# Linear attention and GEGLU on one core: attention's queries turned by VectorE through DRAM, every down projection by seven products, the attention chunks moved

## The chip, the core and the metric

The kernel runs on one core of a Trainium2 chip. The metric is the device time of one execution in microseconds (us). An execution has a span, from the first to the last instruction that the profiler records on the core, and a little time around it. The core has five engines that run side by side, each through its own list of instructions in order: TensorE (PE, matrix products; its weight loads stand as PEld), VectorE (DVE), ScalarE (ACT), GpSimd (POOL) and SyncE (SP). Here SP issues all the DMA transfers, in one queue. [...]

## The reference

x is 2048 tokens by 512 features, float32.

```
xn  = layernorm(x)
q, k, v = split(xn @ wqkv)              # 32 heads of 16
pq, pk  = phi(q), phi(k)                # phi(t) = (t + 1 if t > 0 else exp(t)) + 1e-6
kv  = sum over tokens of pk^T v, z = sum over tokens of pk      # per head
s   = ((pq @ kv) / (pq . z + 1e-6)) @ wo
g   = silu((gelu(xn @ w_gate) * (xn @ w_up)) @ w_down)          # 1792 hidden columns
out = x + s * g
```

## The kernel before

**Precision and tiles.** A float32 product is made from two rounded parts of each factor, high and low: three matrix products (high by high, high by low, low by high) stand for one. `split` makes the parts: ACT copies the high part, DVE (or POOL) subtracts it to leave the low part. Nearly every matrix instruction is a 128x128 weight tile against 512 columns. Most products are made block by block, two by two, with seven products in place of eight (`PRODUCTS`, `prod`, `fprod`, `down_strassen`); the sums and differences that this takes are made by DVE and POOL.

**Stages.** First a QKV stage over the 16 token tiles: layer norm, a transposition of xn by PE, k and q by seven products (the first four tiles by the plain sum), phi, and G = xn^T pk in four PSUM banks (`gps`), from which kv follows later. phi(q) goes to DRAM (`q_d`); the forms of xn for tokens 0 to 1023 go to DRAM too (`xh_d`, `xl_d`), those for tokens 1024 to 2047 stay (`Xh`, `Xl`). Then pass 1 (tokens 1024 to 2047) and, after the attention, pass 0 (tokens 0 to 1023) of the feed-forward net. A pass has seven units of 256 hidden columns. A unit has two quads, gate and up (`quad`): 42 matrix instructions each, into the banks FX, FY and FZ. The weights of a quad (`w`) are cut into their parts once, in pass 1 (`prep_w`), written to DRAM (`w_d`), and loaded from there in pass 0. The products h of units 0 to 4 go through the down projection by seven products (`down_strassen`, keys "E", banks dX, dY and dZ, 42 instructions a unit), with four differences of h (`h_sums`) and seven high and low pairs (`hfh`, `hfl`) a unit. Units 5 and 6 (`SD = 5`) go through a plain sum at the end of the pass (`down`, keys "D", bank d, 48 instructions a unit).

**Attention** stands between the passes, in four chunks of 512 tokens (`attn`). kv and M = kv @ wo are made there (`pkv`, `pm`, `M_hi`, `M_lo`), from G that came back from DRAM. For each of 16 token tiles phi(q) is loaded, POOL multiplies it by z (`u`), DVE sums by head (`den`), adds, takes the reciprocal (`rr`) and scales (`pn`); PE transposes it by products with the identity (`ptq`, 4 instructions for each of 16 pieces); ACT and DVE split it (`pqT`); PE makes s (`sps`, 12 instructions a tile, 16 tiles). Two chunks are multiplied by pass 1's silu there and go out, two go to DRAM (`s_d`) for the end of pass 0.

**The order of the work** isn't the order of the code. Each operation is recorded with its engine, a stated cost and what it reads and writes (`Plan.do`). The order of the matrix products is written out as a list of keys (`pe_keys`); `Plan.order` then simulates the engines with the stated costs, takes for each engine the operation with the earliest latest-start (`late`), and applies the drawn changes of `late` that the table `KEPT` names. What it emits is a fixed list for each engine. Nearly every line in the profile is that of a helper: L486 is any matrix product, L453 any copy of ACT, L459 any `tt` of DVE or POOL, L1024 an addition to `acc`, L449 any DMA.

## Time and profile before

| | |
|---|---|
| three runs | 611.77, 613.39 and 614.51 us; median 613.39 |
| the profiled execution | 613.08 us, of it the span 611.3 |
| PE busy | 604.2 us in 2736 matrix instructions |
| DVE, ACT, POOL busy | 464.9, 334.2 and 211.7 us |
| DMA | 112.70 MB, mean 184 GB/s |

How to read it: matrix instructions overlap in PE, so that one lasts about 390 ns by its row while the next begins 227 ns after it. Busy time counts a stretch in which several overlap once. An idle time stands beside the engine that had it, with what ended it; idle time of an engine that nobody waits for costs nothing. In rows of instructions, `out<-in` names the tiles, buffer numbers left out.

### The profile page before, as it was taken

The numbers are of one execution on the slowest core, as the hardware profiler recorded it, in microseconds if no ns is written. First come the engines' busy times: TensorE is split into PE (matmuls) and PEld (weight loads), VectorE is DVE, ScalarE is ACT, GpSimd is POOL, SyncE is SP. The second block draws the span as 40 slices with busy tenths as digits, with TensorE's granted clock in tenths as the row PEclk, the third lists the DMA queues.
The fourth block names the chain that finished last, engine by engine and source line by source line (L and its number), as shares of the span: only waits on it lengthen the run. The fifth ranks groups of instructions, "written<-read, shape, count | busy, mean of one in ns | idle before, by whom it ended". The sixth has DMA issues, their size and how long they took to land.

```text
span 611.3 us, 7799 instructions
## 1 busy us (share of the span) xinstructions
PE 604.2 (99%) x2736; PEld 497.0 (81%) x2736; DVE 464.9 (76%) x745; ACT 334.2 (55%) x602; POOL 211.7 (35%) x209
## 2 busy tenths in 40 slices
PE   9999999999999999999999999999999999999997
PEld 8887888888888888888888787888887888888886
DVE  6999888677799999999757698714566868686456
ACT  6787877786677464656343322244654535353533
POOL 4456754364453654543013324013031121300110
PEclk9999999999999999999999999999999999999999
DMA  7149921107838354481669795255534344343245
GB/s 260 54 144 310 282 86 57 48 36 293 322 123 328 105 240 159 185 304 71 246 233 397 287 399 198 87 189 192 205 102 174 117 158 154 122 154 122 71 168 192
DMA packets 49079, 112.70 MB, mean 184 GB/s; under 512 B 3088, under 2 KB 24848, under 8 KB 45456
## 3 DMA queue, kind: packets, MB, share of 16 engines
q1 hardware_dynamic: 49040, 112.21, 50.3%
q8 instruction: 21, 0.34, 0.2%
q14 instruction: 18, 0.15, 0.1%
HBM read 67.63 MB, written 44.56 MB: 184 GB/s over the span
## 4 chain that ended last, share of the span: by engine, by line
PE 92%; DVE 5%; DMA 1%; issue 1%; ACT 0%; POOL 0%; SPq 0%; ACTq 0%; POOLq 0%
PE FX L486 24%; PE FZ L486 12%; PE dX L486 9%; PE gps L486 7%; PE d L486 7%; PE FY L486 6%; PE X L486 6%; PE dZ L486 4%; PE Z L486 3%; PE sps L486 3%; PE dY L486 2%; PE k L486 2%; PE q L486 2%; PE Y L486 1%; PE pt L651 1%; PE warm L516 1%
## 5 line engine op out<-in xcount | busy, mean ns | idle before, releaser
L486 PE MATMUL FX<-Xh,w 128*128 128x512 f32 x448 | 134.8, 390 | 0.2 <-ACT fu L453 0.2
L1065 POOL TENSOR_TENSOR h<-h,g 128x512 f32<-128x512 f32 x28 | 38.6, 1377 | 185.2 <-DVE h L459 185.2
L486 PEld LDWEIGHTS FX<-Xh,w 128*128 128x128 f32 x448 | 83.8, 188 | 18.5 <-ACT fu L453 1.3
L486 PE MATMUL FX<-Xl,w 128*128 128x512 f32 x224 | 69.0, 389 | 0.0
L486 PE MATMUL FZ<-Xh,w 128*128 128x512 f32 x224 | 69.0, 389 | 0.0
L453 ACT COPY fu<-FX 128x512 f32<-128x512 f32 x56 | 32.8, 585 | 37.1 <-PE FX L486 36.1
L486 PEld LDWEIGHTS FX<-Xl,w 128*128 128x128 f32 x224 | 42.1, 188 | 8.8
L486 PEld LDWEIGHTS FZ<-Xh,w 128*128 128x128 f32 x224 | 42.1, 188 | 8.7
L1024 DVE TENSOR_TENSOR acc<-acc,dX 128x512 f32<-128x512 f32 x52 | 35.4, 680 | 15.9 <-PE dX L486 15.9
L459 DVE TENSOR_TENSOR h<-fu,FZ 128x512 f32<-128x512 f32 x28 | 19.2, 686 | 30.0 <-ACT fu L453 24.1
L459 POOL TENSOR_TENSOR sums<-draw 128x256 f32<-128x256 f32 x20 | 19.8, 1002 | 51.1 <-DMA draw<-in_B_w_down 27.4
L459 POOL TENSOR_TENSOR tmp<-raw 128x256 f32<-128x256 f32 x28 | 24.6, 889 | 36.2 <-ACT g L989 10.4
L459 POOL TENSOR_TENSOR u<-q,zacc 128x512 f32<-128x512 f32 x16 | 20.8, 1318 | 44.3 <-DMA q<-q_d 31.6
L486 PE MATMUL FZ<-Xl,w 128*128 128x512 f32 x112 | 34.5, 389 | 0.0
L486 PE MATMUL FY<-Xh,w 128*128 128x512 f32 x112 | 34.4, 390 | 0.0
L729 POOL TENSOR_TENSOR zacc<-zacc,kp 128x512 f32<-128x512 f32 x16 | 24.7, 1542 | 27.2 <-DVE kp L718 26.9
L486 PE MATMUL sps<-pqT,M_hi 128*128 128x512 f32 x128 | 32.3, 393 | 0.0
L453 ACT CAST hfh<-sums 128x512 fp32r<-128x512 f32 x40 | 24.3, 621 | 14.1 <-DVE sums L459 13.9
L453 ACT CAST hfh<-h 128x512 fp32r<-128x512 f32 x30 | 18.5, 622 | 24.1 <-DVE h L459 16.3
L486 PE MATMUL dX<-hfh,dh 128*128 128x512 f32 x80 | 31.2, 390 | 0.2 <-ACT dY L453 0.2
L486 PE MATMUL dX<-hfl,dh 128*128 128x512 f32 x80 | 31.2, 390 | 0.0
L459 DVE TENSOR_TENSOR hfl<-sums,hfh 128x512 fp32r<-128x512 f32 x40 | 31.0, 786 | 0.2
(198 smaller groups left out, 1514.6 us busy)
## 6 DMA issues: line engine op xcount, KB each, us to landing
w_d<-w SPq DMA_DIRECT2D x14, 1792.0 KB, 8.5
w<-w_d SPq DMA_DIRECT2D x14, 1792.0 KB, 7.3
draw<-in_B_w_down SPq DMA_DIRECT2D x14, 512.0 KB, 4.3
x<-in_A_x SPq DMA_DIRECT2D x16, 256.0 KB, 3.6
q_d<-qp SPq DMA_DIRECT2D x16, 256.0 KB, 2.1
q<-q_d SPq DMA_DIRECT2D x16, 256.0 KB, 7.6
xh_d<-Xh SPq DMA_DIRECT2D x4, 896.0 KB, 5.3
xl_d<-Xl SPq DMA_DIRECT2D x4, 896.0 KB, 7.2
```

The lines of the kernel that those rows point to most:

```text
L453: do("ACT", act(n, src.psum), lambda o, i: nc.scalar.copy(o, i), dst, src, name=name)
L459: do(eng, c, lambda o, p, q: getattr(e, f"tensor_{op}")(o, p, q), dst, a, b, name=name)
L486: nc.tensor.matmul(o if r is None else o[:, r], a, b, start=first, stop=made == self.passes[r], skip_group_check=self.on or r is not None)
L516: nc.tensor.matmul(o, w, w, start=True, stop=True)
L651: nc.tensor.transpose(o[:, k, :], a[:, k * P:(k + 1) * P], b)
L729: do("POOL", pool(D), lambda o, i: nc.gpsimd.tensor_add(o, o, i), zacc, p0, name="zacc")
L1024: do("DVE", dve(D), lambda o, i: nc.vector.tensor_add(o, o, i), o, ps, name="acc")
L1065: do("POOL", pool(NC), lambda o, i: nc.gpsimd.tensor_mul(o, o, i), h, g, name="h")
```

## The change

It has these parts.

- **q turned by DVE.** phi(q) is written to DRAM with its columns regrouped (the host permutes the q columns of wqkv), so that a tile that is read back has its four quarters of the features in four groups of 32 partitions. After the scaling (`pn`), one DVE instruction transposes the 32x32 squares of a tile (`turn`, a STREAM_TRANSPOSE that writes every fourth element) into a part of the tile `sums`, and a DMA writes it to `t_d`; a chunk is read back from there already turned (`tq`, `pql`, `pqh`). The 64 `ptq` products are gone. The z product, the sums by head and the reciprocals (`den`, into `rall`) are made earlier, and q is loaded twice, once for `den` and once for `turn`. These jobs have due times (`behind`, `DUE`): six `den` and four `turn` in pass 1, ten and twelve in pass 0.
- **All down sums by seven products.** `SD`, `down` and the plain sum are gone; units 5 and 6 of both passes go through `down_strassen`. POOL makes the low parts of unit 6's down weights (`EASED`).
- **The chunks.** One attention chunk (chunk 2) stands between the passes, and its s goes to DRAM; chunks 3, 0 and 1 follow pass 0, mixed at first with its last down products (`between`). Seven down products of pass 1 are moved into the start of pass 0 (`MOVED`). silu of pass 1 goes to DRAM (`g_d`) and is loaded again at the end.
- **kv and M early.** wv and wo are loaded at the start of pass 1, G stays on the chip, kv is made after the first quad's products and M just behind; M's parts go to DRAM (`m_d`) and are loaded twice, before each place that uses them.
- **Three quads' weights early.** Those of quads 11, 12 and 13 are cut in the QKV stage (`prep_early`), written to DRAM, and loaded in pass 1 as they are in pass 0.
- **The table `KEPT`** is another one, with more draws.

The diff, cut to its core (of `KEPT` one line each; the code of kv, M, silu and the loads of X is moved more than changed):

```diff
 KEPT = [
-    (-1, 12, [9000067, 9000070, 9000075, 9000095, 9000115]),
...
+    (100, 115, [30000012, 30000014]),
...
+            if o.due is not None:
+                o.late = min(o.late, o.due)
...
-    q_d = dram_view([S, D], "q_d", NT)
-    s_d = dram_view([D, S // 2], "s_d", NT // 2)
-    g_d = dram_view([P, KT, D], "g_d", KT)
-
-    w_d = dram_view([2 * (F // P // 2), P, 2 * 14 * P], "w_d", 2 * (F // P // 2))
+    q_d = dram_view([NT, KT, P, P], "q_d", NT)
+    g_d = dram_view([D, S // 2], "g_d", NT // 2)
+    t_d = dram_view([KT, P, S], "t_d", NT)
+    s_d = dram_view([D, NC], "s_d", KT)
+    m_d = dram_view([2, P, KT, D], "m_d", 2 * KT)
+
+    w_dram = dram.tile([2 * (F // P // 2), P, 2, 14, P], F32, name="w_d")
+    w_res = [[Res() for _ in range(8)] for _ in range(2 * (F // P // 2))]
+
...
-        dma(q_d(t, slice(t * P, (t + 1) * P)), phi(v, t, "q"), 256)
+        dma(q_d(t, t).map(lambda ap: ap.rearrange("q s e -> s q e")),
+            phi(v, t, "q").map(lambda ap: ap.rearrange("p (q e) -> p q e", e=P)), 256)
...
+    def prep_early(q):
+        raw, t = sums_w(q, R0)
+        for g, src in enumerate(sources(raw, t)):
+            n = GROUPS[g].stop - GROUPS[g].start
+            v = raw_tile(R1, f"we{q}{g}", [P, 2, D]) if g % 2 else None
+            f = [(half(v, hl) if v else tile_in("up", 34 + hl, [P, D], F32, f"we{q}{g}{hl}")).map(
+                lambda ap, n=n: ap.bitcast(F32R).rearrange("p (s c) -> p s c", c=P)[:, 0:n]) for hl in range(2)]
+            split(*f, src, n * P, f"w{g}")
+            for hl in range(2):
+                dma(w_d(q, hl, GROUPS[g], g), f[hl].map(lambda ap: ap.bitcast(F32)), 2 * n * 32)
+
+    EARLY = range(11, 14)
+    WHEN = (90, 140)
+    for n, q in enumerate(EARLY):
+        plan.due = WHEN[0] + (WHEN[1] - WHEN[0]) * n / len(EARLY)
+        prep_early(q)
...
+
+    rall = tile_in("cpool", "zacc", [P, NT, H], F32, "rall", NT)
+
+    def rden(t):
+        return rall.part(rall.res[t:t + 1], (slice(None), t))
+    def den(p, t):
+        q = U("qz", [35], f"qz{t}")
+        dma(rows_of(q), q_d(t, t).map(lambda ap: ap.rearrange("q (s i) e -> (q s) i e", i=KT)), 256)
+        do("POOL", pool(D), lambda o, z: nc.gpsimd.tensor_mul(o, o, z.unsqueeze(1).to_broadcast([P, KT, P])), rows_of(q), zq, name="u")
+        r = rden(t)
+        do("DVE", 0.59, lambda o, i: nc.vector.tensor_reduce(o, i, axis=AX.X, op=ALU.add), r, heads(q), name="den", port=False)
+        do("DVE", 0.11, lambda o, i: nc.vector.tensor_add(o, o, i), r.map(lambda ap: ap.rearrange("p (s h) -> p s h", s=KT)),
+           den_eps.map(lambda ap: ap.unsqueeze(1).to_broadcast([P, KT, H // KT])))
+        do("DVE", 0.28, lambda o: nc.vector.reciprocal(o, o), r, port=False)
...
+        for l, base, w in ((wv, 10, wqkv_k[:, c, 2 * D:3 * D]), (wo_sb, 14, wo[c * P:(c + 1) * P, :])):
+            l.append(tile_in("up", base + c, [P, D], F32, f"wvo{base}{c}"))
+            dma(l[c], ext(w), 256)
+    kv4 = tile_in("up", 18, [P, KT, P], F32, "kv4")
+    pkv = bank(5, "pkv", (P, KT, P))
+    for g in range(KT):
+        def run_kv(o, *ab, g=g):
+            for c in range(KT):
+                nc.tensor.matmul(o[:, g, :], ab[c][:, g * P:(g + 1) * P], ab[KT + c][:, g * P:(g + 1) * P],
+                                 start=(c == 0), stop=(c == KT - 1))
+        do("PE", 0.9, run_kv, pkv, *wv, *GT, key=("kv", g))
+    do("DVE", dve(D), lambda o, i, m: nc.vector.tensor_mul(o, i, m.unsqueeze(1).to_broadcast([P, KT, P])),
+       kv4, pkv, mask2)
+    for g in range(KT):
+        pm = bank([6, 7, 5, 6][g], f"pm{g}")
+        do("PE", 0.9, lambda o, a, b, g=g: nc.tensor.matmul(o, a[:, g, :], b, start=True, stop=True),
+           pm, kv4, wo_sb[g], key=("m", g))
+        m = [tile_in("up", 19 + 2 * g + hl if g < 2 else 25 + 2 * g + hl, [P, D], F32R, f"m{hl}{g}") for hl in range(2)]
+        split(*m, pm, D, "M")
+        for hl in range(2):
+            dma(m_d(KT * hl + g, (hl, slice(None), g)), m[hl].map(lambda ap: ap.bitcast(F32)), 256)
+
+    down_f = w_down.rearrange("(f p) n -> p f n", p=P)
+    FE, FC, FG = range(0, 3), range(3, 6), range(6, 10)
...
+        if q in EARLY:
+            w = ws[q] = tile_in("wp", ring("w", [0, 1, 2]), [P, 2, 14, P], F32R, f"w{q}", 8)
+            dma(w.map(lambda ap: ap.bitcast(F32)), w_d(q), 2220)
+            return
...
+            split(*f, src, n * w, "d", "POOL" if (p, u) in EASED else "DVE")
...
+    def turn(p, t):
+        pn = U("qz", [35], f"q{t}")
+        dma(rows_of(pn), q_d(t, t).map(lambda ap: ap.rearrange("q (s i) e -> (q s) i e", i=KT)), 256)
+        do("DVE", 0.6, lambda o, j: nc.vector.scalar_tensor_tensor(
+            o, o, EPS, j.unsqueeze(2).to_broadcast([P, H, DH]), op0=ALU.add, op1=ALU.mult),
+           heads(pn), rden(t), name="pn")
+        s = spare(p)
+        v = s.part(s.res[8:9], (slice(None), 6)).map(lambda ap: ap.rearrange("p (g c) -> p g c", c=P))
+        do("DVE", 0.6, lambda o, i: nc.vector.transpose(
+            o.rearrange("p g (s t) -> p g t s", t=KT), i.rearrange("p (t g d) -> p g t d", t=KT, d=32)),
+           v, pn, name="turn", port=False)
+        dma(t_d(t, (slice(None), slice(None), slice(t * P, (t + 1) * P))).map(lambda ap: ap.rearrange("g p c -> p g c")), v, 256)
+
...
+    def attn(c, M, place):
+
+        src = View([t_d(t, ()).res[0] for t in range(4 * c, 4 * c + 4)],
...
+                dma(tq[h], src[:, 2 * h:2 * h + 2], 512)
+            tq = [v[:, k] for v in tq for k in range(2)]
+        else:
+            tq = place(0, KT).map(lambda ap: ap.bitcast(F32))
+            dma(tq, src, 1024)
+            tq = [tq[:, k] for k in range(KT)]
         forms_ = []
         for k in range(KT):
-            pt = bank(ring("spt", [0, 1]), f"ptq{c}{k}", (P, 4, P))
-
-            def run_t(o, b, *a, k=k):
-                for j in range(4):
-                    nc.tensor.transpose(o[:, j, :], a[j][:, k * P:(k + 1) * P], b)
-            do("PE", 0.45, run_t, pt, ident, *pns, key=("QT", i, k))
-            ptf = pt.map(lambda ap: ap.rearrange("p j c -> p (j c)"))
-            f = [tile_in("up", places[i % 2][k][hl], [P, NC], F32R, f"pqT{hl}{c}{k}") for hl in range(2)]
-            split(*f, ptf, NC, "pqT")
+            f = [place(KT + 2 * k + hl, 1)[:, 0] for hl in range(2)]
+            split(*f, tq[k], NC, "pqT", "POOL" if c in HELPED else "DVE")
             forms_.append(f)
         for n in range(KT):
-            ps = bank(ring("sps", [3, 4, 2]), f"sps{c}{n}")
-            Sum(ps).add(("S", i, n), *three([[M[hl].part(M[hl].res[k:k + 1], (slice(None), k, slice(n * P, (n + 1) * P))) for hl in range(2)]
-                                             for k in range(KT)], forms_), name="S")
...
+            ps = bank(ring("sps", [3, 4, 2, 0, 1]), f"sps{c}{n}")
+            Sum(ps).add(("S", c, n), *three([[m[:, k, rows] for m in M] for k in range(KT)], forms_), name="S")
+            if c == CHUNKS[0]:
+                so = U("so", FG, f"so{n}")
+                copy("ACT", so, ps, D, "so")
+                dma(s_d(n, rows), so, 256)
+                continue
+            out_tile(c, n, ps)
...
+                g = acc[0, 4 * c + n]
+                silu(g)
             else:
-                so = U("sxr", FACC, f"so{c}{n}")
...
+    def between(p, wait, s):
+
+        out = wait + down_keys(p, NU - 1)
+        for n, (k, at_) in enumerate(zip(s, BETWEEN[p])):
+            out.insert(at_ + n, k)
+        return out
...
+    BETWEEN = {1: (7, 9, 11, 14), 0: (5, 8, 11, 14)}
+    DENS = 6
+    HELPED = (2,)
+    EASED = ((1, 6), (0, 6))
+    MOVED = 7
+    DUE = {1: (150, 320), 0: (355, 530)}
...
+    behind(1, *DUE[1], *[(den, t) for t in TURN[:DENS]], *[(turn, t) for t in TURN[:4]])
...
+    g_take(100)
+    pe_keys += keys[2:5] + ["z"] + keys[5:KV] + [("kv", g) for g in range(KT)] + keys[KV:KV + 3]
+    pe_keys += [("m", g) for g in range(KT)] + keys[KV + 3:]
+    middle = between(1, wait, sums(CHUNKS[0]))
+    moved = middle[len(middle) - MOVED:]
+    pe_keys += middle[:len(middle) - MOVED]
...
+    behind(0, *DUE[0], *[(den, t) for t in TURN[DENS:]], *[(turn, t) for t in TURN[4:]])
+    keys, wait = ffn(0, moved)
+    M = load_m()
+    vs = {hl: tile_in("xf", hl, [P, 14, NC], F32R, f"pq{hl}", 14) for hl in "lh"}
+    for n in range(KT):
+        s = U("g", SPOTS, f"s{n}")
+        dma(s, s_d(n, at(0, n)[0]), 256)
+        out_tile(CHUNKS[0], n, s)
+    for c, hl in zip(CHUNKS[1:], "lhl"):
+        attn(c, M, lambda i, n, v=vs[hl]: v.part(v.res[i:i + n], (slice(None), slice(i, i + n))))
+    pe_keys += keys + between(0, wait, sums(CHUNKS[1])) + sums(CHUNKS[2]) + sums(CHUNKS[3])
```

What PE does between the last quad of pass 1 and the first of pass 0. Before, the plain sums' last tile (d), the transpositions (ptq) and the first attention products (sps):

```order
L486 MATMUL d_5_70_3477<-hh_11_3133,dwh_3068 128x512
L486 MATMUL d_5_70_3477<-hh_11_3058,dwh_3043 128x512
L1241 MATMUL ptq_3523<-ident,pn_3371 128x128
L1241 MATMUL ptq_3523<-ident,pn_3258 128x128
L1241 MATMUL ptq_3523<-ident,pn_3443 128x128
L1241 MATMUL ptq_3523<-ident,pn_3342 128x128
L486 MATMUL d_5_70_3477<-hl_11_3139,dwh_3068 128x512
L486 MATMUL d_5_70_3477<-hl_11_3072,dwh_3043 128x512
L486 MATMUL sps_3545<-pqT_3468,M_hi 128x512
L486 MATMUL sps_3545<-pqT_3501,M_hi 128x512
```

Now, the down products of units 5 and 6 (dX, dY, dZ) and the one chunk of attention, whose split queries stand in rows of Xl:

```order
L559 MATMUL dY_1_3498<-hfh_5_3267,dl_5_3247 128x512
L559 MATMUL dZ_1_3501<-hfh_5_3245,dh_5_3261 128x512
L559 MATMUL sps_3530<-Xl_3458,M_3296 128x512 x4
L559 MATMUL dX_1_3487<-hfh_5_3361,dh_5_3261 128x512
L559 MATMUL sps_3530<-Xl_3458,M_3404 128x512 x4
L559 MATMUL dX_1_3487<-hfl_5_3389,dh_5_3261 128x512
L559 MATMUL dX_1_3487<-hfh_5_3361,dl_5_3300 128x512
L559 MATMUL sps_3530<-Xl_3458,M_3296 128x512 x4
L559 MATMUL dZ_1_3501<-hfh_5_3245,dl_5_3300 128x512
L559 MATMUL sps_3559<-Xl_3458,M_3296 128x512 x8
L559 MATMUL sps_3559<-Xl_3458,M_3404 128x512 x4
```

All four chunks stood there with their transpositions, after the plain sums; now one chunk (48 instructions) and 44 instructions of the down products stand between the two quads, and no transposition.

What SP issues there, before: the attention's loads of q, the weights of the first quad of pass 0, and the rows of Xh:

```order
L449 DMA q_3302<-q_d 128x512
L449 DMA w_3306<-w_d 128x3584
L449 DMA q_3351<-q_d 128x512
L449 DMA q_3379<-q_d 128x512
L449 DMA q_3399<-q_d 128x512
L449 DMA q_3449<-q_d 128x512
L449 DMA Xh_3481<-xh_d 128x1024 x7
```

Now the parts of M, the rows of Xl and Xh and the next quads' weights in one run:

```order
L522 DMA M_3404<-m_d 128x2048
L522 DMA qz_3437<-q_d 128x512
L522 DMA Xl_3458<-xl_d 128x1024 x3
L522 DMA w_3482<-w_d 128x3584
L522 DMA Xh_3489<-xh_d 128x1024 x7
L522 DMA qz_3521<-q_d 128x512
L522 DMA s_d<-so_3557 128x512
L522 DMA s_d<-so_3607 128x512
L522 DMA draw_0_3618<-in_B_w_down 128x2x512
L522 DMA s_d<-so_3644 128x512
L522 DMA w_3661<-w_d 128x3584
L522 DMA Xl_3458<-xl_d 128x1024 x3
```

The rows of Xh moved from the middle of the attention to behind the last quad of pass 1; four rows of Xl hold the split queries and come last (the fourth stands two rows further down).

DVE at the program's end, before: the last tiles are multiplied by acc (L1299) and x is added (L459):

```order
L459 TENSOR_TENSOR fs_5579<-fs_5579,fx_5535 128x512
L1299 TENSOR_TENSOR fs_4022<-fs_4022,acc_2_4279 128x512
L459 TENSOR_TENSOR fs_4022<-fs_4022,fx_5543 128x512
L1299 TENSOR_TENSOR fs_5638<-fs_5638,acc_3_4293 128x512
L459 TENSOR_TENSOR fs_5638<-fs_5638,fx_5605 128x512
L1299 TENSOR_TENSOR fs_5649<-fs_5649,acc_3_4293 128x256
L459 TENSOR_TENSOR fs_5649<-fs_5649,fx_5616 128x256
L1299 TENSOR_TENSOR fs_5649<-fs_5649,acc_3_4293 128x256
L459 TENSOR_TENSOR fs_5649<-fs_5649,fx_5616 128x256
```

Now the last two chunks' tiles (L1351 reads the attention's bank):

```order
L1351 TENSOR_TENSOR acc_2_3996<-acc_2_3996,sps_5731 128x512
L532 TENSOR_TENSOR acc_1_4073<-acc_1_4073,sxr_5725 128x512
L532 TENSOR_TENSOR acc_0_4039<-acc_0_4039,sxr_5729 128x512
L532 TENSOR_TENSOR acc_2_3996<-acc_2_3996,sxr_5742 128x512
L1351 TENSOR_TENSOR acc_2_3996<-acc_2_3996,sps_5755 128x512
L532 TENSOR_TENSOR acc_2_3996<-acc_2_3996,sxr_5707 128x512
L1351 TENSOR_TENSOR acc_3_4013<-acc_3_4013,sps_5775 128x512
L532 TENSOR_TENSOR acc_3_4013<-acc_3_4013,sxr_5752 128x512
L1351 TENSOR_TENSOR acc_3_4013<-acc_3_4013,sps_5792 128x256 x2
L532 TENSOR_TENSOR acc_3_4013<-acc_3_4013,sxr_5717 128x256 x2
```

The same two steps a tile, but all 12 tiles of the three last chunks read their banks here, and the splits of the queries (pql, pqh) and the last additions to acc stand in the rows ahead.

464 lines of the change are left out of this document (232 added, 232 removed).

## The prediction

> **What bounds it now.** I read the page first (busy times, then the shares of the chain that ended last), then what PE waited for, then the chain in order of time, and the busy times by stretch last.
>
> ```profile
> PE 604.2 (99%) x2736; PEld 497.0 (81%) x2736; DVE 464.9 (76%) x745; ACT 334.2 (55%) x602; POOL 211.7 (35%) x209
> PEclk9999999999999999999999999999999999999999
> PE 92%; DVE 5%; DMA 1%; issue 1%; ACT 0%; POOL 0%; SPq 0%; ACTq 0%; POOLq 0%
> ```
>
> ```profile
> PE warm L516 <- DVE neg_half L507: 1.1, 1, 1.1
> PE ptq L1241 <- DVE pn L1231: 1.1, 2, 0.7
> PE FX L486 <- ACT fu L453: 0.2, 1, 0.2
> PE dX L486 <- ACT dY L453: 0.2, 1, 0.2
> ```
>
> PE works 604.2 of 611.3 us at the full granted clock, waits 2.6 us in all, and 92% of the chain is its own. So a matrix instruction that goes is worth its full pace, as long as nothing new makes PE wait. The pace is the start-to-start time, read off the chain:
>
> ```profile
> 165.08 2.72 PE FX L486 x12
> 388.55 0.88 PE ptq L1241 x8
> 389.42 13.61 PE sps L486 x60
> 587.82 19.20 PE d L486 x96
> ```
>
> A 512-column instruction takes 2.72 / 12 = 0.227 us, a transposition 0.88 / 8 = 0.11. The 96 at the end are 72 of 512 columns (16.3 us) and 24 of 256: 2.9 / 24 = 0.12.
>
> ```profile
> 160.00:280.00 120.00, 120.00 (x530) 98.99 (x529) 113.83 (x165) 74.51 (x140) 61.01 (x62) 1.00 0.54 205
> 480.00:560.00 80.00, 80.00 (x354) 66.27 (x353) 57.28 (x91) 36.13 (x65) 14.04 (x13) 1.00 0.43 158
> ```
>
> The third busy time is DVE's. In pass 1 it is busy 113.83 of 120 us (95%; 0.69 us an instruction) and PE still never waits; in pass 0 it is at 72% (0.63 us each). DVE is the engine that this change loads, so the sum has a gain on PE and a charge wherever DVE or the DMA may come late.
>
> **The gain, all on PE.**
>
> ```profile
> L486 PE MATMUL d<-hh,dwh 128*128 128x512 f32 x60 | 18.7, 397 | 0.0
> L486 PE MATMUL d<-hh,dwh 128*128 128x256 f32 x8 | 1.6, 282 | 0.0
> L1241 PE MATMUL ptq<-ident,pn 128*128 128x128 f32 x64 | 9.0, 274 | 1.1 <-DVE pn L1231 1.1
> 352.37 1.09 PE L486 MATMUL sps<-pqT,M_hi 128*128 128x512 f32 x4
> ```
>
> - Down sums of units 5 and 6, both passes: three forms like the first row and three like the second, 180 x 0.227 + 24 x 0.12 = 43.7 us, become 4 units x 42 x 0.227 = 38.1: -5.6 us.
> - 64 transpositions x 0.11: -7.0 us.
> - Gaps in the attention: from the first `sps` at 352.37 to the last at 389.42 + 13.61 = 403.03 are 50.7 us, for 192 x 0.227 + 48 x 0.11 = 48.8 us of work. DVE fed PE there just in time; that stage goes: -1.9 us.
>
> kv and M cost PE what they did (their instructions are the same, only earlier), and so do the 192 `sps`. Against the profiled execution's 613.1 us this leaves 613.1 - 14.5 = 598.6.
>
> **The charges.**
>
> *The last tile.* The two halves of the last tile now come out of one bank after PE has ended, so DVE's two steps run twice in place of once, and the silu is no longer behind PE.
>
> ```profile
> 607.11 0.39 ACT acc L1117
> 607.52 0.44 DVE fs L1299
> 607.98 0.43 DVE fs L459
> ```
>
> Before 1.26 us, now 2 x (0.44 + 0.43) = 1.74: +0.5.
>
> *DVE in pass 1.* In the new order DVE has 300 instructions from the first gate sum of pass 1 to the first of pass 0: seven down units by seven products, ten `den` and `turn` jobs and M's four splits come in, and three quads' weight splits go out. 20 are little ones:
>
> ```profile
> L1227 DVE TENSOR_TENSOR den<-den,den_eps 128x32 f32<-128x32 f32 x16 | 5.2, 332 | 0.2
> 338.25 3.57 PE pkv L1198 x32
> 343.64 2.58 PE pm L1208 x6
> 347.58 0.86 PE pm L1208 x2
> ```
>
> 280 x 0.69 + 20 x 0.33 = 200 us. PE has there 14 quads x 42 + 7 units x 42 - 21 moved on + 48 = 909 x 0.227 = 206.1, with kv and M 213 us: 94%, as full as the stretch that harmed nobody. It isn't even: units 3 and 4 hold 46 and 44 instructions, 62.1 us for 2 x 126 x 0.227 = 57.1 of PE. That is the upper end, +5; the lower is 0, since the same two units held 42 and 41 before (57.3 us) at no cost. I take +1.5, near the row that cost nothing.
>
> *The transposition.* No row shows VectorE writing every fourth element. By the nearest rows it costs between 0.56 and 1.49 us:
>
> ```profile
> L603 DVE TENSOR_SCALAR xn<-x,mv,rstd 128x512 f32<-128x512 f32 x16 | 8.7, 561 | 1.7 <-POOL rstd L599 1.7
> L1024 DVE TENSOR_TENSOR acc<-acc,dX 128x512 f32<-128x512 f32 x52 | 35.4, 680 | 15.9 <-PE dX L486 15.9
> L459 DVE TENSOR_TENSOR kq<-wk,kq 128x1024 fp32r<-128x1024 f32 x2 | 3.0, 1492 | 0.1
> ```
>
> The first is as many elements with one source, the last twice as many with two. I take 0.68, the common price of 512 elements, already in the 0.69. The four of pass 1 could cost 4 x 0.8 = 3.2 us more; the twelve of pass 0 fall three to a unit, where 28% of DVE's 28.6 us, 8 us, stand free. [...]
>
> *The work moved forward.* The three early quads bring 12 splits and 24 stores into 90 to 140 us.
>
> ```profile
> 90.00:140.00 50.00, 50.00 (x228) 40.70 (x227) 36.80 (x56) 38.85 (x72) 24.60 (x24) 1.00 0.13 48
> L453 ACT CAST w<-raw 128x512 fp32r<-128x512 f32 x14 | 8.7, 620 | 4.0 <-PE FZ L486 4.0
> L453 ACT CAST w<-raw 128x256 fp32r<-128x256 f32 x14 | 5.6, 403 | 0.0
> ```
>
> ACT: 9 x 0.62 + 3 x 0.40 = 6.8 on 38.85 of 50; DVE some 7.5 on 36.80; DMA share 0.13. All covered: 0 (to +1, if ACT's 91% makes k late). Moving kv and M forward adds eight loads of 256 KB, eight stores and four loads of 1 MB to SP's queue, ahead of the weights of pass 1's later quads; SP issues 272 transfers for 193. Each is a few tenths, and a quad's weights are asked for a quad ahead: 0.
>
> *The reload between the passes.*
>
> ```profile
> DMA packets 3564, 10.67 MB, mean 395 GB/s; under 512 B 313, under 2 KB 313, under 8 KB 3344
> 60.00:80.00 20.00, 20.00 (x94) 16.21 (x94) 17.74 (x32) 15.51 (x29) 14.43 (x15) 1.00 0.93 271
> ```
>
> The first row is 318 to 345 us: 395 GB/s held for 27 us. Where 512-byte pieces of X are spilled (60 to 80 us) it is 271 at a share of 0.93; `q_d` and `t_d` are now written in such pieces. Ten rows of X at 0.52 MB and a quad's weights at 1.83, 7.1 MB, follow the last quad of pass 1: 17.9 us at 395 (26.1 at 271). PE has 92 instructions, 20.9 us, before it needs the first. +1 between 0 and 26.1 - 20.9 = +5.2; I stay near 0 because large pieces ran at 395.
>
> *The end.* After the last quad PE has 199 instructions, 45.1 us, and DVE 67 whole ones and 4 halves: 67 x 0.63 + 4 x 0.43 = 43.9. Before, DVE had 25 left there. Any lag that DVE brings along, or a load that comes late in its list, now shows. About 14.3 MB of turned q, silu, x and output move there, 318 GB/s: 36 us at 395, 53 at 271. So 0 to 53 - 45 = +8; at 0.69 an instruction DVE would be 2.8 longer. I take +2.5, by that.
>
> Sum: 598.6 + 0.5 + 1.5 + 0 + 1 + 2.5 = 604.1. The profiled execution lies 0.3 below the runs' median, so 604.4.
>
> **Rivals.**
>
> A. The forecast, 604.4; with its small charges from nothing to double, 600 to 609. Chance 0.55.
>
> B. Everything stays covered: 598.6 + 0.5 + 0.3 = 599.4. For it: PE waits 2.6 us in the whole trace with DVE at 95%. Against: the end leaves DVE no room. 0.12.
>
> C. The turn costs two rows of 0.68: four of them in the full stretch of pass 1, 4 x 0.68 = 2.7 us, on A: 607.1. [...] 0.10.
>
> D. The gain is eaten by DMA: at 271 GB/s at both places, 5.2 + 7.7 instead of 1 + 2.5: 613.8, no change. For it: the new 512-byte pieces, and more bytes at both places. Against: the loads there are in pieces of 2 KB and more. 0.10.
>
> E. DVE becomes the bound in pass 1, and the kernel is slower. Its instructions get dearer when POOL reads beside them:
>
> ```profile
> L459 DVE TENSOR_TENSOR sums<-h,sums 128x512 f32<-128x512 f32 x20 | 16.3, 813 | 0.1
> L459 DVE TENSOR_TENSOR dl<-sums,dh 128x512 fp32r<-128x512 f32 x20 | 16.5, 831 | 12.7 <-ACT dh L453 12.7
> ```
>
> If the mean went to the 0.813 of the first row, 280 x 0.813 + 6.6 = 234 us, 21 beyond PE's 213: 598.6 + 0.5 + 21 + 2.5 + 0.3 = 623. PE waits from (213 - 6.6) / 280 = 0.74 on, and from about 0.79 the gain is gone. Against: the mean with all these rows in it is 0.69, and POOL gets less weight work in pass 1. 0.13.
>
> A measurement of this kernel can tell about 0.5%, 3.1 us, from no change. Faster by more (below 610.3): A, B and C, 0.77. Within: D, 0.10. Slower: E, 0.13. The range leaves out E and a little below B: 599.2 to 614. A alone is 600 to 609.
>
> **What the profile after would show.** PE at about 590 us busy in some 100 fewer instructions, no `ptq` and no `d` rows, and the first `FX` of pass 0 some 21 us after the last of pass 1. PE's waits, 2.6 us now, at 4 to 8, with `hfl` or `pqT` parts of DVE and loads of X as releasers; DVE near 95% until pass 1 ends. STREAM_TRANSPOSE at 0.7 us speaks for the sum, at 1.3 for C. PE waiting on `Xh`, `Xl` or `w` at the start of pass 0 is D; on `hfl`, `w` or `acc` through pass 1 is E. The forecast is wrong if the waits of PE sum to more than 12 us.

## The result, and the profile after

The changed kernel takes 607.27 us (median of 6 runs, 605.7 to 609.89) beside 613.24 us of the kernel before (median of 6): a ratio of 0.991, with an interval of 0.988 to 0.994. So it is 0.9% faster, 6.0 us, where 9.0 us were forecast. The profiled execution took 607.62 us with a span of 605.6 us. Its busy times, the shares of the chain that ended last, and what PE waited for:

```profile
PE 596.0 (98%) x2636; PEld 483.1 (80%) x2636; DVE 516.7 (85%) x819; ACT 351.8 (58%) x631; POOL 243.3 (40%) x237
PE 88%; DVE 7%; ACT 2%; DMA 1%; issue 1%; POOL 1%; SPq 0%; DVEq 0%; POOLq 0%
```

```profile
PE dX L559 <- DVE acc L1182: 1.5, 2, 0.9
PE warm L589 <- DVE neg_half L580: 1.1, 1, 1.1
PE dX L559 <- DVE hfl L532: 0.8, 1, 0.8
PE k L559 <- DVE kq L532: 0.3, 1, 0.3
PE dZ L559 <- DVE acc L1182: 0.3, 1, 0.3
PE FX L559 <- DVE w L532: 0.3, 1, 0.3
PE X L559 <- DVE Xl L532: 0.2, 1, 0.2
PE dX L559 <- ACT dY L526: 0.2, 1, 0.2
```

PE has 100 instructions less and waits 4.7 us for 2.6; 4 to 8 were forecast. The view of waits counts only what is left of a wait after the instructions in flight have run out, though: one lasts 0.39 us by its row and the next begins 0.227 us after it, so the first 0.16 us of a delay don't show. The full account needs PE's start-to-start times. I took them from all of PE's rows and subtracted the prediction's paces (0.227 us for 512 columns, 0.12 for 256, 0.11 for the smaller ones); what is left is PE's loss. Each column is one profiled execution.

| stretch (us) | PE's work, before / after | PE's loss, before / after |
|---|---|---|
| up to the first k | - | 8.4 / 8.0 |
| first k to the first FX of pass 1 | 122.4 / 123.7 | 2.4 / 3.1 |
| pass 1, to its last quad | 189.3 / 196.5 | 0.2 / 3.3, of it 1.6 at pm |
| between the passes | 76.8 / 20.9 | 3.4, of it 1.6 at pm / 1.1 |
| pass 0, to its last quad | 183.9 / 193.0 | 0.9 / 4.1 |
| after the last quad | 19.1 / 44.7 | 0.0 / 2.5 |
| behind PE's last start | - | 4.6 / 4.9 |
| sum | 591.5 / 578.8 | 19.8 / 26.8 |

(Each of the eight `pm` takes 0.43 us from start to start, 0.2 more than the pace taken here; it was so before, and it moved with M into pass 1.) Where PE's order is the same, the losses of pass 1 repeat from kernel to kernel (3.2 to 3.3 us in six of those below), while those of the stretch before it vary from 3.0 to 3.7. The work fell by 12.7 us; that is the count of instructions at these paces, and that the paces hold shows where PE loses next to nothing (0.2 us in 189 of work, pass 1 before). The loss grew by 7.0, and 3.2 of that are in pass 0, where the prediction had charged nothing. The experiments ask what these losses are.

Two of them stand out in the trace. The first, from the timeline (start and length in us, engine, line, what ended the wait ahead of it):

```profile
387.08 1.31 POOL L1035 TENSOR_TENSOR qz<-qz,zq 128x512 f32<-128x512 f32 x1
387.17 1.77 DVE L532 TENSOR_TENSOR sums<-h,h 128x512 f32<-128x512 f32 x1 [1.48 <-POOL h L1222]
390.72 2.17 DVE L532 TENSOR_TENSOR hfl<-sums,hfh 128x512 fp32r<-128x512 f32 x2
391.16 1.18 POOL L532 TENSOR_TENSOR sums<-draw 128x256 f32<-128x256 f32 x1
392.94 0.50 PE L559 MATMUL dX<-hfl,dh 128*128 128x512 f32 x1 [0.81 <-DVE hfl L532]
```

A den job's product started on POOL 0.09 us before DVE's `sums`, which took 1.77 us for its usual 0.69. The two `hfl` that follow it took 1.03 and 1.21 us for 0.69 beside POOL's steps on the down weights, and PE's dX, which reads the second of them, came 1.09 us late. The second is a part of the chain that ended last:

```profile
426.09 7.36 DMA qz<-q_d
433.58 1.30 POOL qz L1035
437.39 0.96 PE dX L559 x3
```

and in the timeline DVE's wait beside it:

```profile
434.90 0.69 DVE L1037 TENSOR_REDUCE rall<-qz 128x32 f32<-128x512 f32 x1 [3.09 <-POOL qz L1035]
```

SP had issued a load of weights, 1.8 MB, at 425.68 us, just ahead of the q load of a den job. That one took 7.36 us, DVE stood 3.09 us at the job's sum, with `hfl` and the `acc` that frees PE's bank dX queued behind it, and PE was 1.03 us late. What the prediction named as doubtful, the turn, among the costliest groups, and then the busy times by stretch (PE, weight loads, DVE, ACT, POOL, then clock, DMA share and GB/s):

```profile
L1288 DVE STREAM_TRANSPOSE sums<-q 128x512 f32<-128x512 f32 x16 | 17.6, 1102 | 0.3
```

```profile
160.00:333.00 173.00, 172.55 (x754) 140.32 (x754) 158.25 (x248) 98.55 (x181) 74.05 (x75) 1.00 0.61 221
334.00:357.00 23.00, 22.68 (x98) 17.75 (x98) 17.76 (x28) 11.97 (x20) 12.55 (x10) 1.00 1.02 389
440.00:553.00 113.00, 112.82 (x495) 92.39 (x494) 101.18 (x155) 51.52 (x92) 27.72 (x28) 1.00 0.59 200
```

A turn takes 1.10 us. In pass 1 DVE is busy 91%, in most of pass 0 90%, where it was 72% before. Between the passes DMA ran at 389 GB/s, and PE waited for no row of X there and for no weights.

### The profile page after: what moved, and what is told of

The parts are those of the page before. It is cut to its first block, busy times and chain, and to the rows that moved or that the text cites. A ratio compares the mean times of both kernels' runs of the same rounds, so it can differ in the third digit from the quotient of the medians.

```text
span 605.6 us, 7877 instructions
## 1 busy us (share of the span) xinstructions
PE 596.0 (98%) x2636; PEld 483.1 (80%) x2636; DVE 516.7 (85%) x819; ACT 351.8 (58%) x631; POOL 243.3 (40%) x237
## 4 chain that ended last, share of the span: by engine, by line
PE 88%; DVE 7%; ACT 2%; DMA 1%; issue 1%; POOL 1%; SPq 0%; DVEq 0%; POOLq 0%
PE FX L559 21%; PE dX L559 11%; PE FZ L559 11%; PE sps L559 7%; PE gps L559 7%; PE FY L559 6%; PE dZ L559 6%; PE X L559 5%; PE dY L559 3%; PE Z L559 2%; PE q L559 2%; PE k L559 2%; DVE acc L1182 1%; DMA qz<-q_d 1%; PE Y L559 1%; PE pt L724 1%
## 5 line engine op out<-in xcount | busy, mean ns | idle before, releaser
L1182 DVE TENSOR_TENSOR acc<-acc,dX 128x512 f32<-128x512 f32 x76 | 51.7, 680 | 18.3 <-PE dX L559 18.0
L526 ACT CAST hfh<-sums 128x512 fp32r<-128x512 f32 x56 | 34.5, 622 | 51.2 <-DVE sums L532 50.7
L559 PE MATMUL dX<-hfh,dh 128*128 128x512 f32 x112 | 44.1, 395 | 1.7 <-DVE acc L1182 1.5
L559 PE MATMUL dX<-hfl,dh 128*128 128x512 f32 x112 | 43.9, 392 | 0.8 <-DVE hfl L532 0.8
L1035 POOL TENSOR_TENSOR qz<-qz,zq 128x512 f32<-128x512 f32 x16 | 23.2, 1447 | 52.0 <-DMA qz<-q_d 48.2
L532 DVE TENSOR_TENSOR hfl<-sums,hfh 128x512 fp32r<-128x512 f32 x56 | 41.0, 740 | 3.3 <-ACT hfh L526 2.6
L559 PE MATMUL dX<-hfh,dl 128*128 128x512 f32 x112 | 43.5, 392 | 0.1
L1182 DVE TENSOR_TENSOR acc<-acc,dZ 128x512 f32<-128x512 f32 x52 | 35.5, 682 | 7.8 <-PE dZ L559 7.5
L526 ACT CAST hfh<-h 128x512 fp32r<-128x512 f32 x42 | 25.9, 620 | 19.5 <-DVE h L532 10.7
L532 DVE TENSOR_TENSOR sums<-h,h 128x512 f32<-128x512 f32 x28 | 25.1, 897 | 10.6 <-POOL h L1222 10.6
```

Of the source, the lines that this page charges most:

```text
L526: do("ACT", act(n, src.psum), lambda o, i: nc.scalar.copy(o, i), dst, src, name=name)
L532: do(eng, c, lambda o, p, q: getattr(e, f"tensor_{op}")(o, p, q), dst, a, b, name=name)
L559: nc.tensor.matmul(o if r is None else o[:, r], a, b, start=first, stop=made == self.passes[r], skip_group_check=self.on or r is not None)
L1035: do("POOL", pool(D), lambda o, z: nc.gpsimd.tensor_mul(o, o, z.unsqueeze(1).to_broadcast([P, KT, P])), rows_of(q), zq, name="u")
L1182: do("DVE", dve(D), lambda o, i: nc.vector.tensor_add(o, o, i), o, ps, name="acc")
```

## The experiments

Each kernel ran beside the kernel before, whose median was 612.6 to 613.2 us in these runs. The losses are PE's, counted as above, in one profiled execution of each. e2, e4, e5 and e11 change what is computed and serve only to read a cost. Where an experiment needed another order, the order stands in it as a fixed list.

| | us | ratio to before | loss in pass 1 / between / pass 0 / after |
|---|---|---|---|
| changed kernel | 607.27 | 0.988 to 0.994 | 3.3 / 1.1 / 4.1 / 2.5 |
| e1, SP as written | 606.99 | 0.987 to 0.992 | 3.2 / 1.1 / 2.8 / 1.5 |
| e2, no change of table | 607.67 | 0.989 to 0.993 | 3.3 / 1.1 / 3.9 / 1.1 |
| e3, turn twice | 622.07 | 1.012 to 1.017 | 5.4 / 1.1 / 17.0 / 2.3 |
| e4, turn flat | 606.50 | 0.987 to 0.991 | 2.7 / 1.1 / 3.5 / 2.3 |
| e5, SP as written, small u | 603.52 | 0.983 to 0.986 | 2.8 / 1.1 / 2.1 / 1.1 |
| e6, no draws | 609.60 | 0.994 to 0.997 | 3.9 / 1.2 / 2.1 / 3.8 |
| e7, before with unit 5 by seven | 624.51 | 1.018 to 1.021 | 1.6 / 9.2 / 2.3 / 2.0 |
| e8, no early weights | 609.07 | 0.993 to 0.995 | 4.5 / 1.2 / 2.5 / 3.4 |
| e9, own draws | 607.49 | 0.990 to 0.993 | 2.7 / 1.1 / 2.7 / 2.7 |
| e10, SP as written, u later | 604.96 | 0.984 to 0.989 | 3.3 / 1.1 / 1.9 / 1.0 |
| e11, SP as written, small x | 605.93 | 0.986 to 0.991 | 3.3 / 1.1 / 3.1 / 1.0 |
| e12, as e10, start undrawn | 604.51 | 0.984 to 0.989 | 3.3 / 1.1 / 1.9 / 1.1 |

### The q load behind the weights (e1)

The order of four engines is kept as the plan has it; SP isn't among them, and seven of its 272 transfers are issued in another order than the plan's, this q load among them.

```diff
-ENGINES = {mybir.EngineType.PE, mybir.EngineType.Activation, mybir.EngineType.DVE, mybir.EngineType.Pool}
+ENGINES = {mybir.EngineType.SP, mybir.EngineType.PE, mybir.EngineType.Activation, mybir.EngineType.DVE, mybir.EngineType.Pool}
```

> SP's transfers in the written order. In the changed kernel SP issued a load of weights (w, 1.8 MB, at 425.68 us) one place ahead of the q load of a den job (qz, at 426.09), which landed after 7.36 us; DVE stood 3.09 us before that job's sum, and PE 1.03 us behind it at 436 us. Theory (pass 0 lost its 3.2 us to two single late arrivals, not to DVE's load): with the q load first it lands in about 3 us, DVE's 3.09 us and PE's stall at 436 us go, 607.3 - 1.1 = 606.2 us. Rival (DVE is short of time in all of pass 0, so a stall that is taken away comes back later in the same pass): the stall at 436 us goes, PE's last instruction still ends near 601 us, 607.3 us.

The timeline of e1, its SP queue and DVE:

```profile
426.21 0.32 SPq L522 DMA_DIRECT2D qz<-q_d  x1
426.63 0.37 SPq L522 DMA_DIRECT2D w<-w_d  x1
432.30 0.68 DVE L1037 TENSOR_REDUCE rall<-qz 128x32 f32<-128x512 f32 x1
```

The q load goes first and lands at 428.95 us, DVE takes the sum without a wait, and PE's stall at 436 us is gone. The other six transfers stand ahead of 145 us. Pass 0 loses 2.8 us for 4.1, and nothing of it comes back later in the pass: the theory holds in the trace. In the medians, 606.99 beside 607.27 where 606.2 was expected, it can't be told from the scatter.

### The tables of ACT (e2)

One difference that I hadn't looked for: ACT loads a table 11 times, before 5 times. Eight of the loads start between 352 and 384 us, seven of them in the first quads of pass 0, since pass 1's last silu come between pass 0's gelu. Two rows of the changed kernel's timeline:

```profile
369.11 1.28 ACT L1361 ACT_TABLE_LOAD   x1
371.06 1.28 ACT L1147 ACT_TABLE_LOAD   x1
```

```diff
-            silu(g)
+            silu(g, AF.Gelu_apprx_tanh)
```

> The eight silu of pass 1 are gelu here (the function is another, the instruction and its place are the same), so ACT need not change its table between 352 and 385 us, where the changed kernel loads a table eight times of 1.28 us. Theory (PE's 1.09 us at 391 us come from the gelu of the first unit of pass 0 behind those loads): 2 to 3 table loads in the whole trace for 11, ACT 11 us less busy there, PE's stalls between 356 and 395 us fall from 1.6 us to under 0.4, 606.0 us. Rival (DVE's rate in pass 0): table loads go, the stall at 391 us stays or moves a unit on, 607.3 us.

ACT was busy 21.75 us between 360 and 400 for 29.97, and the gelu ahead of the stall came 1.4 us sooner, at 383.79 us. The stall stayed: 0.86 us for 1.09. POOL's `h` behind that gelu also needs DVE's sum from the bank FZ, which was done at 385.8 us, no sooner than before (385.7). So the tables were in view but not in the way, and my theory on them was wrong.

### How much room DVE has (e3, e4)

```diff
-        do("DVE", 0.6, lambda o, i: nc.vector.transpose(
+        do("DVE", 0.6, lambda o, i: [nc.vector.transpose(
             o.rearrange("p g (s t) -> p g t s", t=KT), i.rearrange("p (t g d) -> p g t d", t=KT, d=32))
+            for _ in range(2)],
```

> Each of the 16 turns is made twice: 16 x 1.10 = 17.6 us more on DVE, 4.4 of them in pass 1 (where DVE is at 91 to 94%) and 13.2 in pass 0. Theory (DVE has slack at both places, as the prediction's rivals C and E took it: 8 us a unit free in pass 0): under 2 us slower, 607.5 to 609. Rival (DVE's rate bounds pass 1 or pass 0): the part of the 17.6 us that falls into a full stretch comes out one for one, 4 us or more, 611 to 625.

The rival holds, and by far. Of the 4.4 us added to DVE in pass 1, 2.1 came out on PE; of the 13.2 in pass 0, 12.9. The time rose by 14.8 us. DVE had stood idle 11.8 us between 440 and 553 us in the changed kernel, but in pieces, waiting for PE (6.0 us), POOL (3.5) and ACT (1.5); in the fixed order little of the added work went into them. PE's largest waits in e3:

```profile
PE dX L559 <- DVE acc L1182: 4.9, 5, 1.4
PE dX L559 <- DVE hfl L532: 3.9, 3, 2.5
PE dX L559 <- ACT dY L526: 2.2, 1, 2.2
```

The longest of them in its timeline:

```profile
519.68 0.50 PE L559 MATMUL dX<-hfl,dh 128*128 128x512 f32 x1 [2.52 <-DVE hfl L532]
```

The busy times of e3 in the stretch behind it:

```profile
521.00:525.00 4.00, 4.00 (x12) 3.17 (x11) 3.88 (x7) 0.99 (x2) 0.00 (x0) 0.57 0.42 115
```

About 1.7 us of the loss in pass 0 are of another kind: after that wait the granted clock fell to a half for 3.4 us, and PE's starts stood 0.43 us apart in place of 0.227. The wait of 2.2 us for `dY`, which ended at 552.8 us, had no such sequel: the clock stayed at 1.00.

```diff
-            o.rearrange("p g (s t) -> p g t s", t=KT), i.rearrange("p (t g d) -> p g t d", t=KT, d=32)),
+            o.rearrange("p g (t s) -> p g t s", t=KT), i.rearrange("p (t g d) -> p g t d", t=KT, d=32)),
```

> The turn writes its 512 columns one beside the other in place of every fourth (the tokens inside a tile of 128 then stand in another order, so that s meets other tokens' g; all instructions and transfers stay). If the step of 16 bytes is what a turn costs above 0.68 us, its mean falls from 1.10 to about 0.68 us, DVE is 6.7 us less busy, and the time falls by 0 to 0.5 us where DVE has slack, by up to 2 where it hasn't. If the transposition itself costs 1.10, nothing changes.

The turn in e4's groups:

```profile
L1288 DVE STREAM_TRANSPOSE sums<-q 128x512 f32<-128x512 f32 x16 | 11.3, 708 | 0.3
```

The step of four elements costs 0.39 us a turn; written side by side, a turn takes 0.71 us, about as much as this trace's other steps of 512 elements (`sums<-h,sums` 0.71, `acc<-acc,dX` 0.68). Taking these 6.3 us from the turns gives PE 0.5 us in pass 1 and 0.6 in pass 0; DVE as a whole is only 2.5 us less busy (514.2 for 516.7), and other steps of it last longer (`dl<-sums,dh` 0.76 us in the mean for 0.69). So the order stands at an edge: work added to DVE comes out nearly whole in pass 0 (12.9 of 13.2 us) and by half in pass 1 (2.1 of 4.4), work taken away hardly shows (1.1 of 6.3).

### POOL beside DVE (e5, e10)

```diff
-lambda o, z: nc.gpsimd.tensor_mul(o, o, z.unsqueeze(1).to_broadcast([P, KT, P])), rows_of(q), zq, name="u")
+lambda o, z: nc.gpsimd.tensor_mul(o[:, 0, 0:32], o[:, 0, 0:32], z[:, 0:32]), rows_of(q), zq, name="u")
```

> SP as written, and besides POOL multiplies 32 columns in place of 512 in each of the 16 den jobs (the rest of phi(q) goes into the sums without z, so the sums by head are others); DVE's instructions are the same. In the changed kernel and with one table, POOL's product qz ran from 387.08 us beside DVE's sums<-h,h, which took 1.77 us in place of 0.69, and PE's dX came 1.09 us late behind it at 391.6. Theory (in pass 0 DVE's two-source steps stand still while POOL works, and the den jobs' products are what POOL works on): that step takes 0.7 us, PE's stall at 391 us falls under 0.3, pass 0 loses under 1.7 us (2.78 with SP as written), 606.0 us. Rival (the stall is the chain of the first unit itself): 1.0 us stay at 391, 607.0 us.

The stall at 391 us fell to 0.2 us, pass 0 loses 2.1 us for 2.8 of e1 (under 1.7 was expected), and the kernel is 3.5 us faster than e1 with intervals that don't meet. DVE has the same instructions and is 8.4 us less busy, 510.7 for 519.1. The spans of the two profiled executions differ by 1.8 us, and only 0.7 of it lie in pass 0; 0.4 lie in pass 1 and 0.4 after the last quad. What is left of the 3.5 isn't explained.

The traces show what POOL does to DVE everywhere. In the changed kernel 54 of DVE's TENSOR_TENSOR steps of 128x512 with both sources in SBUF start while POOL is in a TENSOR_TENSOR, over 0.1 us before its end: 51 of them end 0.54 to 0.56 us after POOL's, up to 1.79 us long, and three take 0.66 to 0.68 us. The other 258 take 0.63 to 0.70 us, and of 92 that start beside POOL but have one source in a PSUM bank none takes longer than 0.70 us. DVE stands 25 us longer in this way, 10.5 of them in pass 1 and 3.8 in pass 0; before it was 28, with 17.2 and 4.4. In e5 it is 5.1 and 1.9.

The product can't be left out of a kernel that is to be right, but it can stand elsewhere:

```diff
 POOL: h (385.84)
-      u of den job 6 (387.08)
       four steps on the down weights (389.63 to 393.5)
+      u of den job 6
       u of den job 7
 DVE:  ...
-      den, its sum and reciprocal of job 6 (392.81, 394.61, 395.38)
       hfl of the next unit (397.75)
+      den, its sum and reciprocal of job 6
 SP:   ...
-      load of q for job 7 (393.51)
       w (397.12)
+      load of q for job 7
```

> SP as written, and one den job of pass 0 later in the lists: POOL's product qz that ran at 387.08 us beside DVE's sums<-h,h comes after POOL's four steps on the down weights, its three DVE steps after the next unit's first low part, and the load and product of the den job behind it follow. Nothing else moves, the result is the reference's. Theory (that product alone made PE late at 391 us): the stall there falls from 1.0 to under 0.4, pass 0 loses about 2.0 us for 2.78, the kernel is 0.5 to 1.0 us faster than with SP as written, 606.0. Rival (POOL's steps on the down weights, or the product in its new place, stop DVE as long): the stall stays or moves to 394 to 400 us, 607.0.

The same place in e10's timeline:

```profile
387.17 0.69 DVE L532 TENSOR_TENSOR sums<-h,h 128x512 f32<-128x512 f32 x1 [1.47 <-POOL h L1222]
393.46 1.75 POOL L1035 TENSOR_TENSOR qz<-qz,zq 128x512 f32<-128x512 f32 x1
393.97 1.78 DVE L532 TENSOR_TENSOR hfl<-sums,hfh 128x512 fp32r<-128x512 f32 x1
```

In its old place the step of DVE takes 0.69 us again, and PE's loss at 391 us is 0.09. The product now stops another DVE step, at 393.97 us, and nobody waits for that one. Pass 0 loses 1.9 us, as expected, and the end 1.0. The median is 604.96 us, and all its runs lie below all runs of e1 and of the changed kernel, though the intervals of the ratios meet; nothing of the work is left out. It is 2.0 us below e1 where 0.5 to 1.0 were expected: in the two traces 0.9 of it is pass 0, 0.5 the end and the rest lies ahead of pass 1, where nothing was changed.

### The end (e11)

```diff
-                tt("DVE", "add", o, o, xr[:, cs], w)
+                tt("DVE", "add", o[:, 0:32], o[:, 0:32], xr[:, cs][:, 0:32], w)
```

> SP as written, and the 16 additions of x at the end are made on 32 columns in place of 512 (the rest of x isn't added): DVE has 16 x 0.55 = 8.8 us less to do after the last quad. Theory of the prediction (DVE's rate costs the end 2.5 us): what PE loses after the last quad of pass 0, 2.48 us in the changed kernel and 1.51 with SP as written, falls under 0.5, and the last steps behind PE are 0.3 shorter, 605.5. Rival (the loss there is single waits at the joint of the last unit and the attention, before DVE's load at the end matters): 1.0 to 2.5 us stay, 606.5 to 607.

The busy times behind the last quad in e1:

```profile
553.00:599.00 46.00, 45.35 (x198) 36.37 (x197) 43.47 (x69) 17.86 (x31) 5.71 (x5) 1.00 0.79 273
```

and in e11, with the small additions:

```profile
553.00:599.00 46.00, 45.36 (x200) 36.86 (x198) 36.46 (x69) 17.77 (x31) 6.03 (x5) 1.00 0.83 280
```

DVE was relieved of 7 us, and PE's loss is 1.0 us, the same as in e10, where DVE has all its work. The median, 605.93 us, lies between the two expectations. 0.8 of the loss is one wait in all of these kernels (555.3 us in the changed one): PE's next dX needs a bank that DVE's `acc` has just begun to read. The rest, up to 1.5 us in the changed kernel, are mostly waits of `sps` and the down products beside it for ACT's high parts of the first queries and of h; they come and go between kernels whose end is the same, so they depend on what arrives from pass 0. Only e4 lost time late in the end, 1.0 us at 582 us behind DVE. The rival holds by the traces: the loss at the end is at the joint, not DVE's rate.

### Parts of the change by themselves (e7, e8, e9, e6, e12)

Down sums by seven products alone, for one unit more in the kernel before (e7):

```diff
-    SD = {1: 5, 0: 5}
+    SD = {1: 6, 0: 6}
```

> The kernel before, with unit 5 of both passes by seven products too and unit 6 alone by the plain sum (SD = 6), the drawn changes of the order found anew: one part of the change by itself, in part. PE has 2 x 1.4 = 2.8 us less work. Theory of the prediction's sum (a matrix instruction that goes is worth its pace): 613.2 - 2.8 = 610.4, up to 612. Rival (the plain sums were what PE did while DVE made the last unit's forms; by seven products the end of a pass needs other work beside it, which the changed kernel has in the attention chunk): PE waits several us at the end of each pass, slower than before, 615 to 622 us.

PE's work fell by the 2.8 us, and the time rose by 11.9. The stretch between the passes lost 9.2 us (before 3.4), and 7.8 us lay behind PE's last start for 4.6; the other stretches lost some 6 us more. The busy times of that stretch in the kernel before:

```profile
318.00:403.00 85.00, 83.93 (x410) 68.71 (x409) 62.57 (x116) 24.37 (x41) 22.83 (x19) 1.00 0.72 269
```

and in e7:

```profile
318.00:410.00 92.00, 87.85 (x416) 68.78 (x415) 70.20 (x133) 28.03 (x48) 23.98 (x19) 1.00 0.74 265
```

PE's waits in e7:

```profile
PE ptq L1241 <- DVE pn L1231: 1.5, 2, 1.3
PE ptq L1241 <- DVE pqT L459: 1.1, 2, 0.9
```

DVE has 17 instructions more there, and PE waits at the transpositions for DVE's `pn` and `pqT`. The rival holds: in the order found for it, this part alone costs more than it gains. That it pays in the changed kernel because the transpositions are gone and the attention is spread fits, but wasn't tried part by part.

Without the early weights (e8), and for comparison the changed kernel with draws found by the same search (e9):

```diff
-    EARLY = range(11, 14)
+    EARLY = range(0)
```

> The changed kernel without the early weights (EARLY empty: quads 11 to 13 are cut in pass 1 again), its order with draws found anew by the same number of tries as the next run. About 3 x 3.0 = 9 us of DVE's splits go back from the QKV stage to pass 1. Theory (DVE's work in pass 1 is at its limit, 0 to 2 us from PE's): 4 to 9 us slower than the next run. Rival (the early weights moved work from one covered place to another): within 1.5 us of it.

```diff
-KEPT = [
-    (100, 115, [30000012, 30000014]),
...
+KEPT = [  # draws found anew, fewer
```

> The changed kernel with nothing else changed than its drawn changes of the order, found anew with as many tries as in the run without early weights, fewer than the kernel's own table had: what that one is compared with. If only the sum of stalls counts, it lies 0 to 4 us above the changed kernel, 607 to 611.

e8 takes 609.07 us and e9 607.49: 1.6 us, with intervals of 0.993 to 0.995 and 0.990 to 0.993, which just meet. It lies between the two expectations, at the edge of the rival's and far from the theory's. Pass 1 loses 4.5 us for 2.7, so the difference is where the theory put it, with a fifth of the 9 us that DVE got back there.

```diff
-KEPT = [
-    (100, 115, [30000012, 30000014]),
...
-    (500, 560, [30059945]),
-]
+KEPT = [
+]
```

> The changed kernel with the table KEPT empty: the order that the planner makes by itself, without the drawn changes. Theory (the change lives by an order in which nearly every late arrival is tuned away, since DVE has no slack in either pass): PE's stalls grow by 5 to 9 us, 612 to 616, no faster than before. Rival (the order matters little, the gain is the work taken from PE): 608 to 610.

609.60 us: the rival holds. The drawn order is worth 2.3 us; 3.4 us below the kernel before (612.96 beside it) are there without it. The end loses 3.8, but pass 0 only 2.1, and that says more on the stall at 391 us. The same place in e6's timeline:

```profile
388.62 1.76 DVE L457 TENSOR_TENSOR sums<-h,h 128x512 f32<-128x512 f32 x1 [1.47 <-POOL h L1147]
391.06 0.69 DVE L457 TENSOR_TENSOR hfl<-sums,hfh 128x512 fp32r<-128x512 f32 x1
```

The product stops DVE's `sums` here as in the changed kernel, and PE loses nothing. POOL's steps on the down weights come only at 396.7 us, so both `hfl` behind take 0.69 us; besides, PE comes to that place 0.7 us later against DVE. So the product alone wasn't the cause: its 1.1 us and the 0.9 us of the steps on the weights together made PE 1.09 us late, and either one by itself would have cost PE some 0.2 us at most (an estimate from these numbers).

```diff
 EMIT = [
-    the first 208 steps as drawn
+    the first 208 steps as planned
```

> The last version (SP as written, the one product later) with the first 208 steps, up to about 29 us, in the order that the planner makes without the drawn changes. In the changed kernel PE lost 0.6 us at 10.0 us (k behind DVE's kq) and 0.3 at 15.4, which the kernel before and the one without draws don't lose. Theory (the 0.7 us that the QKV stage loses more than before come from its drawn order and not from the early weights): PE's loss between its first k and the first FX falls from 3.0 to about 2.2 us, 604.2. Rival (the early weights, prepared between 90 and 140 us, cost it): 3.0 us stay, 605.0.

The loss from the first k to the first FX is 2.5 us for 3.0, in the theory's direction but short of its 2.2; the 0.6 us at 10.0 us are gone. But the first k itself starts 0.8 us later (8.75 us for 7.98), so nothing is won in this trace, and the median, 604.51 us, can't be told from e10's 604.96. What clears the early weights is the stretch in which they are made: from 90 us to the first FX PE lost 0.4 us in the changed kernel and 0.5 before.

## Why the prediction came out as it did

The sign, the range and the mechanism (work off PE, charged with DVE arriving late) were right; the median lies 2.9 us above the forecast, and one term that stands at nothing makes up nearly all of that. By its steps:

- **The gain.** 5.6 + 7.0 = 12.6 us of work were forecast, 12.7 counted. The attention's gaps gave 1.7 us for 1.9. A matrix instruction that goes was worth its pace.
- **The last tile.** +0.5 forecast, +0.2 measured.
- **DVE in pass 1.** +1.5 forecast; the loss there grew by 3.3 - 0.2 - 1.6 for pm = 1.4 us, most of it behind late steps of DVE (`dl` at 178 us, `w` at 278). The size and the kind were right.
- **The transposition.** Taken at 0.68 us, it costs 1.10, between the rows 0.56 and 1.49 and between A and C. In pass 1 its extra 0.39 us by four are worth 0.5 us (e4), not the 3.2 of the upper end. Of the 1.10 us the step of four elements is 0.39 (e4).
- **Work moved forward.** 0 to +1 forecast, nothing measured where it is done (0.4 us lost from 90 us on, 0.5 before). What it does for pass 1 was worth 1.6 us (e8 beside e9).
- **The reload.** +1 forecast, and 1.1 us lost there, but not for the reason given. The transfers ran at 389 GB/s and no PE instruction waited for X or w; PE lost it among pass 1's last down products, 0.6 us of it at 335.8 behind DVE's `acc`. That the size fits is luck. D didn't happen at either place: at the end 260 GB/s were moved with the DMA busy 77%, and no wait of PE there is for a load.
- **The end.** +2.5 forecast, 2.5 measured, by luck: the cause is not DVE's rate (e11) but waits at the joint, and kernels with the same end lost 1.0 to 2.5.
- **Pass 0: the step that failed.** It was charged nothing, in two sentences: that the turns "fall three to a unit, where 28% of DVE's 28.6 us, 8 us, stand free", and, said of pass 1, that the transfers put into SP's queue are "a few tenths" each. It lost 3.2 us more than before. The free 28% were those of the kernel before; two more units by seven products, twelve turns at 1.10 us with their scaling and ten den jobs bring DVE to 90% there, and then no slack is left (e3). The ten den jobs of pass 0 had no price at all in the sum. Two of them make 2.2 of the 3.2 us, each by its neighbour and not by its own length: one waits for q behind 1.8 MB of weights (e1), one lets POOL stop a DVE step on PE's path, together with POOL's steps on the weights (e10, e6). The last 1.0 us is in small pieces. With both put right, the kernel takes 604.96 us, where the forecast was 604.4; that it comes so close is partly luck, since the end then lost 1.0 us and not 2.5.
- **The rivals.** B would have needed every stage covered. E named POOL beside DVE as the danger, in pass 1 and as a dearer mean (21 us). POOL costs DVE less in pass 1 now than before (10.5 us for 17.2), as the argument against E had it; it struck PE in pass 0, as one late step. C's doubled turn, two rows of 0.68, was the author's estimate, and it came a little over half true: 1.10 us.

PE was to be busy about 590 us and was 596: its busy time counts the first 0.16 us of every delay as work, so a forecast of the work can't be read off it.

## What to carry to other kernels

When work is moved onto an engine, price each stage with its load after the change, and count every small job that comes with it, its load and its helper on another engine too. On an engine at 90% in a fixed order, idle time in pieces is little room: doubling the turn showed it at once (12.9 of 13.2 us came out on PE in pass 0), and is a cheap trial before a new order is searched. Look at what each late arrival stood beside, in the DMA queue and on POOL, since putting two jobs in other places (607.27 to 604.96 us) was worth as much as all the drawn changes (609.60 to 607.27).

## What the runs showed of the hardware

- POOL held up single DVE steps. Of the 54 in the changed kernel that had two sources in SBUF and started over 0.1 us before the end of one of POOL's TENSOR_TENSOR, 51 ended 0.54 to 0.56 us after that end; the other three took 0.66 to 0.68 us, and none of the 92 with a source in PSUM took longer than 0.70 us. The step at 387.17 us ended 0.55 us after the product (1.77 us long for 0.69, product 387.08 to 388.39), the one at 393.97 us in e10 0.54 us after it (1.78 us long, product to 395.21). So these two engines meet not only at semaphores: PE's loss at 391 us was 1.09 us with the product beside that step and 0.09 with the product elsewhere (e10). The prediction took the danger as a rate; what it does here is to make single steps late.
- A wait of PE cost more than its length: in 9 of the 12 places in the changed kernel where a start came over 0.25 us late, the next start came 0.11 us late as well (0.108 us after the 1.09 at 391.6, 0.110 after the 1.03 at 436.1).
- A wait of 2.5 us in e3, which ended at 519.68 us, was followed by 3.4 us at half the granted clock (0.57 in the mean from 521 to 525 us), with PE's starts 0.43 us apart for 0.227. The next longest, 2.2 us in e3 to 552.8 us, left the clock at 1.00; what told the two apart isn't shown.
- ACT's table loads took 1.28 us each, and eight of them in 33 us cost the kernel nothing that could be measured: 607.27 us with them and 607.67 in e2.
